# A two-layer transformer block with routed feed-forward on one core: routing steps moved, normalisation steps paired, a subtraction moved behind the statistics

## The chip, the cores and the metric

The kernel runs on one core of a Trainium2 chip. The metric is device microseconds of one execution; the kernel before takes 4644.64 us (median of three runs, 4642.4 to 4648.78). The core has five engines that each take their own instructions in order: TensorE (PE, with weight loads as PEld), VectorE (DVE), ScalarE (ACT), GpSimd (POOL) and SyncE (SP, which here only starts transfers). An engine that waits for something holds up everything written behind it for the same engine.

## The reference, cut to what matters

Two attention layers and two feed-forward layers alternate on x, 2048 tokens of 1024 numbers:

```python
x = x + A(layernorm(x));  x = x + B(layernorm(x))     # and the same two once more
# A: 32 heads of 32, full softmax attention over 2048 tokens, then @ wo
# B: r = x @ w_r; the 8 tokens with the largest r go through
#    y = (silu(x_sel @ w_gate) * (x_sel @ w_up)) @ w_down;  y *= sigmoid(r_sel)
#    result: x, with y added in the 8 rows
```

## The kernel before

Tokens lie in 16 tiles of 128 rows. `layer(n, ...)` is written once and run for n = 0 and n = 1. It has three stages: the projection to q, k and v (`steps`), the attention loop, and the output projection (`for t in range(NT)` at L1141), which also computes the layer norm that B needs and the router's score per token. Matrix products that need accuracy are made of three products of a high and a low part: ACT casts the high part, and DVE or POOL subtracts it from the whole to get the low one.

**The output projection.** For each tile t, PE makes 48 products (L1157) into a two-bank PSUM tile `pre`, of which there are two. DVE then adds the residual (L1168), scales the attention output of tile t+2 (`scale_o`, L1093), subtracts its low part (`split_o`, L1102, which waits for ACT's cast L1101), takes statistics (`ln_stats`, L141 to L146; the last two instructions, the reciprocal root `rs`, are POOL's), normalises (L1188) and makes the router's score (L1192). L1192 writes its unused product into `pre`, so the buffer comes free only when it is done. POOL makes the factors that are stored for later (L1182 to L1185) and adds x and its normalised value (L1193). At t = 0 DVE also makes the reciprocals of the second half of the softmax sums (L1002) in the memory that becomes `xn`.

**Routing of layer 0.** The feed-forward of layer 0 is spread over layer 1's projection. The 8 tokens are chosen in two stages, one over tiles 0 to 8 (`CT` = 9), one over the rest. Each is the generator `stage`, whose yields cut it in pieces; a piece is issued with `next`. The last piece computes positions `ab`, gathers 8 rows from DRAM with an indirect DMA on POOL's queue and scatters them to other rows of the same tensor, which moves the chosen rows to the end of their half. The first stage's pieces are issued inside the product loop of tiles 10, 11 and 12, the second stage's at steps k = 3 to 8 of layer 1's projection, one per step. At k = 9 the routed rows are normalised (L346) and transposed (L349) for the feed-forward. `permutation` (k = 13 and 17) multiplies three columns out to 8x8 tiles `vb` (L357), which PE transposes (L358).

**The hand-over.** Layer 1 is a generator too (`nxt`). While layer 0 finishes tiles 9 to 15, `next(nxt)` issues its first loads, the statistics and normalisation (`ln_stat`, `ln_norm`, L712) of its first four tiles, the split of its first weight block (`split_w`, cast L694, POOL's subtraction L697) and, after tile 15's products, the transposes of its first two tiles (`ln_tr`, L731, with the low parts on DVE, L739). Its loads of the tokens read the tensor that the scatter writes.

**Layer 1's projection.** Step k makes 24 products (L760), evacuated by ACT's cast (L774) and DVE's subtraction (L775) from three one-bank PSUM buffers `st`. Every second step splits the next weight block. In the first 24 steps, steps 8, 12, 16 and 20 also issue statistics and normalisation of a later tile. Every fourth step issues four pieces of the feed-forward (`tick`, L489 and L518) with the loads of its weights.

## Time and profile before

| | us |
|---|---|
| median of three runs | 4644.64 |
| profiled execution, time | 4644.15 |
| profiled execution, span from first to last instruction | 4642.1 |
| PE busy | 4520.6 (97%) |
| DVE, ACT, POOL busy | 3183.7, 2428.9, 3219.2 |
| mean granted TensorE clock | 0.988 |

An engine's timeline has one row for a run of like instructions: start, length, engine, line, operation, result and operands, and in brackets how long the engine had been idle before it and what ended that idle time. The chain that ended last says nothing here of the middle of the kernel, so the idle time of PE, which is busy 97% of the span, is the thing to read, stage by stage.

### The profile page before, as it was taken

How to read it: one execution, taken by the hardware profiler on the slowest of the kernel's cores; microseconds unless marked ns; L12 is line 12 of the kernel's file. 1: busy time of each engine (PE TensorE's matmuls, PEld its weight loads, DVE VectorE, ACT ScalarE, POOL GpSimd, SP SyncE). 2: the span in 40 equal slices, each digit the busy share in tenths (PEclk: the TensorE clock that was granted, in tenths of full speed). 3: DMA queues.
4: the chain of work that ended last, by engine and by line, in shares of the span. 5: the costliest groups of instructions: out<-in, count | busy, mean ns of one | idle time of the engine just before them, and what ended most of it. 6: DMA issues, size and time to landing. Idle time of an engine off the chain costs nothing. (4 is left out here: it accounts for less than half of the span.)

```text
span 4642.1 us, 73520 instructions
## 1 busy us (share of the span) xinstructions
PE 4520.6 (97%) x29224; PEld 2688.0 (58%) x29224; DVE 3183.7 (69%) x4945; ACT 2428.9 (52%) x2568; POOL 3219.2 (69%) x1247
## 2 busy tenths in 40 slices
PE   9999999999999999989899999999999999999896
PEld 7888755555555555448667786555555555554572
DVE  2211588888888888876422215888888888887763
ACT  3322267676767667750122222776676767677400
POOL 4444288988989898844433342988888899898441
PEclk9999999999999999999899999999999999999997
DMA  6757477776877777658489774777777768676597
GB/s 202 207 175 209 131 162 168 156 174 143 179 153 158 171 153 169 158 139 230 133 289 291 236 216 129 164 158 165 160 161 160 171 147 180 150 169 159 150 250 310
DMA packets 329301, 833.50 MB, mean 180 GB/s; under 512 B 44118, under 2 KB 159830, under 8 KB 279790
## 3 DMA queue, kind: packets, MB, share of 16 engines
q1 hardware_dynamic: 275214, 476.95, 35.0%
q0 software_dynamic: 45216, 325.57, 34.6%
q10 hardware_dynamic: 8528, 26.29, 2.2%
q8 instruction: 229, 3.75, 0.3%
q14 instruction: 114, 0.93, 0.1%
HBM read 384.24 MB, written 119.37 MB: 108 GB/s over the span
## 5 line engine op out<-in xcount | busy, mean ns | idle before, releaser
L639 DVE TENSOR_REDUCE nm<-st 128x1 f32<-128x512 f32 x3916 | 2433.7, 683 | 374.0 <-PE st L631 368.2
L1031 ACT ACTIVATE P<-pre 128x1024 f32<-128x1024 f32 x2048 | 1986.2, 1022 | 720.8 <-PE pre L646 522.2
L967 POOL TENSOR_TENSOR acc<-acc,P 128x2048 f32<-128x2048 f32 x434 | 2103.8, 4848 | 80.4 <-DMA P<-P 72.5
L646 PE MATMUL pre<-q,ks 64*128 64x512 f32 (+1 forms) x8192 | 1142.7, 396 | 4.3 <-ACT P L1031 4.3
L957 PE MATMUL pv<-P,v 128*32 128x512 f32 x8192 | 1091.9, 605 | 5.1 <-DMA v<-vd 5.1
L631 PEld LDWEIGHTS st<-ks,q 64*128 64x128 f32 x3916 | 546.5, 184 | 906.6 <-DVE nm L639 764.7
L631 PE MATMUL st<-ks,q 64*128 64x512 f32 x3916 | 980.6, 469 | 0.4
L646 PEld LDWEIGHTS pre<-q,ks 64*128 64x128 f32 (+1 forms) x8192 | 770.8, 186 | 190.7 <-ACT P L1031 57.4
L970 POOL DMA_DIRECT2D P<-P x310 | 296.4, 956 | 264.1 <-PE st L631 193.0
L775 DVE TENSOR_TENSOR lo<-st,hi 128x512 fp32r<-128x512 f32 x128 | 88.5, 691 | 568.4 <-ACT hi L774 562.7
L697 POOL TENSOR_TENSOR ohl<-wraw,ord 128x2048 fp32r<-128x2048 f32 x48 | 220.6, 4597 | 338.0 <-ACT ord L694 329.4
L697 POOL TENSOR_TENSOR wl<-wraw,wh 128x2048 fp32r<-128x2048 f32 (+1 forms) x49 | 221.1, 4512 | 303.8 <-ACT wh L694 285.0
L774 ACT CAST hi<-st 128x512 fp32r<-128x512 f32 x128 | 75.4, 589 | 564.1 <-PE st L760 564.1
L957 PEld LDWEIGHTS pv<-P,v 128*32 128x32 f32 x8192 | 161.8, 108 | 261.6 <-issue 253.3
L967 POOL TENSOR_TENSOR acc<-P 128x2048 f32<-128x2048 f32 x62 | 294.7, 4753 | 9.1 <-ACT P L1031 9.1
L1157 PE MATMUL pre<-woh,ohl 128*128 128x512 f32 x1024 | 245.3, 398 | 25.9 <-DVE pre L1192 14.4
L1157 PEld LDWEIGHTS pre<-woh,ohl 128*128 128x128 f32 x1024 | 195.9, 192 | 72.5 <-issue 17.2
L760 PE MATMUL st<-xh,wh 128*128 128x512 f32 x512 | 201.2, 393 | 0.0
L760 PE MATMUL st<-xh,wl 128*128 128x512 f32 x512 | 199.5, 390 | 0.0
L760 PE MATMUL st<-xl,wh 128*128 128x512 f32 x512 | 199.3, 389 | 0.0
L1101 ACT CAST ohl<-ord 128x1024 fp32r<-128x1024 f32 x32 | 33.6, 1051 | 309.6 <-DVE ord L1093 184.7
L760 PE MATMUL st<-woh,ord 128*128 128x512 f32 x512 | 166.8, 401 | 0.0
(344 smaller groups left out, 3866.7 us busy)
## 6 DMA issues: line engine op xcount, KB each, us to landing
P<-P POOLq DMA_DIRECT2D x310, 1024.0 KB, 8.8
wraw<-in_A_wqkv_dram SPq DMA_DIRECT2D x96, 1024.0 KB
q<-qh SPq DMA_DIRECT2D x256, 128.0 KB
ks<-kh SPq DMA_DIRECT2D x112, 256.0 KB
vd<-vn SPq DMA_DIRECT2D x32, 512.0 KB
qh<-hi SPq DMA_DIRECT2D x64, 256.0 KB
ql<-lo SPq DMA_DIRECT2D x64, 256.0 KB
kh<-hi SPq DMA_DIRECT2D x64, 256.0 KB
```

Source lines behind the costliest of these rows:

```text
L631: pe.matmul(ps[b], Q[u][rows, i, 0, qt * 128:(qt + 1) * 128], KS[(u // QC) % 2][rows, i, 0, j * 512:(j + 1) * 512], start=True, stop=True, ...
L639: dve.tensor_reduce(NM[u][:, j, 2 * i + b:2 * i + b + 1, qt], ps[b], axis=AX.X, op=OP.max, negate=True)
L646: pe.matmul(p[:, b * 512:(b + 1) * 512], KS[(u // QC) % 2][rows, i, slot, kt * 128:(kt + 1) * 128], Q[u][rows, i, slot, :], start=(slot == ...
L697: pool.tensor_tensor(wl[:, sl], raw[:, sl], wh[:, sl].bitcast(F32), op=OP.subtract)
L760: pe.matmul(p, *pair(a, l, r), start=(a == 0 and k == 0), stop=(a == KD - 1 and k == 2))
L774: act.copy(hi, p)
L775: dve.tensor_tensor(lo, p, hi.bitcast(F32), op=OP.subtract)
L957: pe.matmul(PV[u][32 * h:32 * h + 32, :], V[g][:, kt, 32 * h:32 * h + 32], P[s][:, h, :], start=(kt == 0), stop=(kt == NT - 1), tile_posit ...
L967: (dve if on_dve else pool).tensor_tensor(o, a, P[u * NT + k].rearrange("p h c -> p (h c)"), op=OP.add)
L970: pool.dma_start(P[u * NT + a], P[u * NT + b], accum_op=OP.add)
L1031: act.activation(P[s][:, 2 * i:2 * i + 2, :].rearrange("p h c -> p (h c)"), p, AF.Exp, scale=SCALE)
L1157: pe.matmul(p[:, bl], l[:, a, :], r[a][:, bl], start=(k == 0 and a == 0), stop=(k == 2 and a == KD - 1))
```

## The change

1. `stage` yields once more: the gather is issued in one piece, the scatter in the next. The first stage's pieces start one tile earlier (tile 9, last of the loop, then tiles 10, 11, and 12 at its third part's start), and the scatter is issued at tile 12 after the statistics. In the second stage the scatter comes at k = 9 and the routed rows at k = 10, so the feed-forward's pieces (`tick`, `refill`) come one step later too.
2. `permutation` makes `vb` on DVE.
3. `split_o` casts at once, and DVE's subtraction L1102 is issued after `ln_stats`, in both layers.
4. In the hand-over the statistics of layer 1's tiles 0 and 1 are issued together at tile 13, behind that tile's own statistics, their normalisations at its end; those of tiles 2 and 3 likewise at tile 14. Nothing is left of them at tile 15.
5. In layer 1 the low part of the first two weight blocks is subtracted in four instructions instead of one.
6. The small tiles `bst`, `mv` and `rs` are three deep instead of two, and an unused tile `pad` is shorter by 32 columns.

```diff
-        st = small.tile([128, 2, 6], F32, name="bst")
+        st = small.tile([128, 2, 6], F32, name="bst", bufs=3)      # mv and rs likewise
...
             self.gather(tg, abi[:, 0:1], dst)
-            self.scatter(abi[:, 1:2], tg, dst)
...
+            yield
+            self.scatter(abi[:, 1:2], tg, dst)
...
-                pool.tensor_scalar(vb, ones_c[:, 0:8], PERM[i]["v"][:, j:j + 1], None, op0=OP.mult)
+                dve.tensor_scalar(vb, ones_c[:, 0:8], PERM[i]["v"][:, j:j + 1], None, op0=OP.mult)
...
-                for i in range(parts):
-                    sl = slice(2048 // parts * i, 2048 // parts * (i + 1))
+                sls = [slice(2048 // parts * i, 2048 // parts * (i + 1)) for i in range(parts)]
+                for sl in [slice(0, 2048)] if n else []:
                     act.copy(wh[:, sl], raw[:, sl])
-                    if n:
-                        yield
+                    yield
+                for sl in sls:
+                    if not n:
+                        act.copy(wh[:, sl], raw[:, sl])
                     pool.tensor_tensor(wl[:, sl], raw[:, sl], wh[:, sl].bitcast(F32), op=OP.subtract)
...
                 ln_stat(0)
+                ln_stat(1)
+                yield
                 ln_norm(0)
-                yield
-                first_w = split_w()
+                ln_norm(1)
+                first_w = split_w(4)
                 next(first_w)
                 yield
-                ln_stat(1)
-                ln_norm(1)
-                yield
+                ln_stat(2)
+                ln_stat(3)
                 list(first_w)
                 load_w(blocks[2][1])
                 yield
-                ln_stat(2)
-                ln_stat(3)
                 ln_norm(2)
                 ln_norm(3)
...
-                    list(split_w())
+                    list(split_w(4 if n else 1))
...
-                    if k % 4 == 2 and k >= 10:
+                    if k % 4 == 3 and k >= 11:
                         for _ in range(4):
                             prev.tick()
-                    if k % 4 == 3:
+                    if k % 4 == 0:
                         prev.refill()
...
                 act.copy(oh, raw)
-                dve.tensor_tensor(ol, raw, oh.bitcast(F32), op=OP.subtract)
+                def low():
+                    dve.tensor_tensor(ol, raw, oh.bitcast(F32), op=OP.subtract)
+                return low
...
-                        if first_stage and t > CT and k == 2 and a in (0, 6):
+                        if first_stage and k == 2 and (t - CT, a) in ((0, 7), (1, 0), (1, 6), (2, 0), (2, 6), (3, 0)):
                             next(first_stage, None)
-                        if nxt and t >= NT - 3 and (k, a) == (2, 0):
-                            next(nxt)
...
-                if nxt and t in (NT - 4, NT - 1):
+                if nxt and t == NT - 1:
                     next(nxt)
...
-                if t + 2 < NT:
-                    split_o(t + 2)
+                low = split_o(t + 2) if t + 2 < NT else None
...
-                if nxt and t >= NT - 2:
+                if nxt and t == NT - 1:
                     next(nxt)
                 mv, rs = ln_stats(x2)
+                if low:
+                    low()
+                if first_stage and t == CT + 3:
+                    list(first_stage)
+                    next(nxt)
+                if nxt and NT - 3 <= t < NT - 1:
+                    next(nxt)
...
                 dve.scalar_tensor_tensor(waste, xn, 1.0, wrb, op0=OP.mult, op1=OP.mult, accum_out=rcols[:, t:t + 1])
+                if nxt and NT - 3 <= t < NT - 1:
+                    next(nxt)
...
-                if nxt and t in (CT, NT - 3):
+                if nxt and t == CT:
                     next(nxt)
```

More of the change, by code (lines that the diff above doesn't have):

```diff
@@ L98, in tile_kernel @@
     pool.memset(mone, -1.0)
-    cons.tile([128, 48], F32, name="pad")
+    cons.tile([128, 16], F32, name="pad")
     ones32 = cons.tile([128, 32], F32, name="ones32")
@@ L138, in ln_stats @@
     def ln_stats(xt):
-        st = small.tile([128, 2, 6], F32, name="bst")
+        st = small.tile([128, 2, 6], F32, name="bst", bufs=3)
         for i in range(2):
             dve.bn_stats(st[:, i, :], xt[:, i * 512:(i + 1) * 512])
-        mv = small.tile([128, 2], F32, name="mv")
+        mv = small.tile([128, 2], F32, name="mv", bufs=3)
         dve.bn_aggr(mv, st)
-        rs = small.tile([128, 1], F32, name="rs")
+        rs = small.tile([128, 1], F32, name="rs", bufs=3)
         pool.tensor_tensor(rs, mv[:, 1:2], eps_c, op=OP.add)
@@ L310, in stage @@
             dve.tensor_tensor(ab[:, 1:2], ab[:, 1:2], tcol, op=OP.add)
-            abi = perm["ab"] = cons.tile([8, 2], I32, name=f"ab{i}")
+            abi = cons.tile([8, 2], I32, name=f"ab{i}")
             dve.tensor_copy(abi, ab)
@@ L320, in stage @@
             else:
+                perm["ab"] = abi
                 dve.tensor_copy(v[:, 0:1], s)
+            yield
+            self.scatter(abi[:, 1:2], tg, dst)
         def absolute(self, out, pos2):
@@ L1126, in layer @@
                     store_sum(NU - 1, last_sum, rest[:, 512:1024])
-                    split_o(0)
+                    split_o(0)()
                 eng = pool if a in (4, 6) else dve
                 eng.tensor_tensor(wol[a], WOR[:, a, :], woh[a].bitcast(F32), op=OP.subtract)
-            split_o(1)
+            split_o(1)()
             second = XN[0:64, 0:512]
```

## The prediction

> **What bounds the kernel.** I read the page first, then who made PE wait in the two stretches around the output projections (2030 to 2560 us, 4260 to 4642 us), then the timelines of each engine there.

> ```profile
> span 4642.1 us, 73520 instructions
> PE 4520.6 (97%) x29224; PEld 2688.0 (58%) x29224; DVE 3183.7 (69%) x4945; ACT 2428.9 (52%) x2568; POOL 3219.2 (69%) x1247
> ...
> PE st L349 <- DVE fw L346: 11.1, 1, 11.1
> PE st L358 <- POOL vb L357: 9.9, 4, 4.6
> PE pre L1157 <- DVE pre L1192: 8.1, 3, 3.8
> PE st L731 <- DVE woh L739: 7.2, 1, 7.2
> PE st L235 <- DVE fy L232: 1.6, 1, 1.6
> PE pv L489 <- ACT fy L497: 1.2, 1, 1.2
> ...
> PE pre L1157 <- DVE pre L1192: 6.3, 4, 2.8
> ```

> PE idles only 121 us of 4642 (4642.1 - 4520.6). The first six waits (total, times, longest) lie in the first stretch, the last row in the second. The change touches nothing in the attention loop, so its gain must come out of about 45 us of waits, and of what follows a wait: a slower PE.

> ```profile
> 2047.58 3.92 PE L1157 MATMUL pre<-woh,ohl 128*128 128x512 f32 x16 [2.42 <-DVE ohl L1102]
> 2069.81 9.13 PE L1157 MATMUL pre<-woh,ohl 128*128 128x512 f32 x32 [3.81 <-DVE pre L1192]
> ...
> 2147.68 7.42 PE L1157 MATMUL pre<-woh,ohl 128*128 128x512 f32 x32
> ...
> 2158.56 7.42 PE L1157 MATMUL pre<-woh,ohl 128*128 128x512 f32 x32
> ...
> 2209.53 9.12 PE L1157 MATMUL pre<-woh,ohl 128*128 128x512 f32 x32 [2.56 <-DVE pre L1192]
> ...
> 2223.97 7.52 PE L1157 MATMUL pre<-woh,ohl 128*128 128x512 f32 x32 [1.70 <-DVE pre L1192]
> ...
> 2243.63 1.12 PE L731 MATMUL st<-ident,xt 128*128 128x128 f32 x4 [7.20 <-DVE woh L739]
> ```

> An undisturbed tile takes PE 10.88 us (2158.56 - 2147.68). The same 32 products take 7.42 us after no wait, 7.52 after 1.70 us, but 9.12 after 2.56 us: a wait of 2.56 us or more costs 1.7 us on top. After 2.42 us, 16 products took 3.92, little over half of 7.42. The price starts between 2.42 and 2.56 us, and I count half of it (0.85) for a wait that I forecast at about 2.5. [...]

> **DVE in one tile.**

> ```profile
> 2149.02 1.22 DVE L1093 TENSOR_TENSOR ord<-ord 128x1024 f32<-128x1024 f32 x1
> 2151.41 1.23 DVE L1102 TENSOR_TENSOR ohl<-ord,ohl 128x1024 fp32r<-128x1024 f32 x1 [1.17 <-ACT ohl L1101]
> 2152.55 1.28 DVE L141 BATCH_NORM_STATS2 bst<-x 128x6 f32<-128x512 f32 x2
> ...
> 2155.01 0.81 DVE L1188 TENSOR_SCALAR xn<-x,mv,rs 128x1024 f32<-128x1024 f32 x1 [0.93 <-POOL rs L146]
> 2155.86 1.23 DVE L1192 SCALAR_TENSOR_TENSOR pre<-xn,wrb 128x1024 f32<-128x1024 f32 x1
> ...
> 2158.76 1.23 DVE L1168 TENSOR_TENSOR x<-pre,x 128x1024 f32<-128x1024 f32 x1 [1.61 <-PE pre L1157]
> ```

> From one L1168 to the free buffer DVE needs about 9.3 us (L1168 and L1093 1.15 each from start to start, the wait, and 5.7 from 2151.41 to L1192's end), of which 1.17 is a wait for the cast and 0.93 one for POOL's root. Behind the statistics, the subtraction finds the cast done, and the root can run beside it: 7.2 to 8.1 us. I take 8, because POOL and DVE hold each other up (below). Against 10.88 us of PE this is hidden in ordinary tiles before and after: worth nothing in tiles 3 to 9. It counts only where DVE is late.

> **Tile 0's reciprocal.**

> ```profile
> 2059.86 3.34 DVE L1002 RECIPROCAL xn<-xn 64x512 f32<-64x512 f32 x1
> ...
> 2067.52 0.81 DVE L1188 TENSOR_SCALAR xn<-x,mv,rs 128x1024 f32<-128x1024 f32 x1 [2.95 <-DMA rd<-xn]
> ```

> L1188 overwrites the memory that L1002's result is being stored from, and waits 2.95 us for that store. With L1102 (1.15) and its wait (1.2) behind it, the reciprocal starts 2.35 us earlier, the store too, and PE's 3.81 us at tile 2 becomes about 1.5, short enough not to slow the clock: 2.35 + 1.65 = **4.0**. The second layer has the same wait, 2.8 us at most (the longest of its row); of it 1.3 to 2.4 goes, by whether the store or PE is last: **1.9**.

> **Tiles 10 to 15 of layer 0.**

> ```profile
> 2198.15 0.95 POOL L209 DMA_INDIRECT fw<-x,ab  x1 [1.48 <-DVE v L321]
> 2205.44 0.89 POOL L213 DMA_INDIRECT x<-fw,ab  x1 [6.34 <-DMA fw<-x,ab]
> ...
> 2207.24 0.81 DVE L1188 TENSOR_SCALAR xn<-x,mv,rs 128x1024 f32<-128x1024 f32 x1 [3.78 <-POOL rs L146]
> ...
> 2208.00 1.74 SPq L78 DMA_DIRECT2D xt<-x  x4
> ...
> 2211.37 1.29 DVE L141 BATCH_NORM_STATS2 bst<-xt 128x6 f32<-128x512 f32 x2 [1.99 <-DMA xt<-x]
> ...
> 2226.90 4.60 POOL L697 TENSOR_TENSOR ohl<-wraw,ord 128x2048 fp32r<-128x2048 f32 x1
> ...
> 2226.97 5.08 DVE L712 TENSOR_SCALAR xt<-xt,mv,rs 128x1024 f32<-128x1024 f32 x1 [1.76 <-POOL rs L146]
> ...
> 2242.16 0.81 DVE L712 TENSOR_SCALAR xt<-xt,mv,rs 128x1024 f32<-128x1024 f32 x1 [0.44 <-POOL rs L146]
> ```

> At tile 10, PE waits 1.6 us for a piece that was issued only 12 products earlier; spread by one tile, the piece finds its inputs made, unless a small DVE operation is held by POOL: **1.0** (0 to 1.6).

> At tile 12, POOL stands 6.34 us in front of the scatter, and tile 12's root is queued behind it. So L1188 is 3.78 us late, and PE waits 2.56 us at tile 14. Now the root comes first, and only POOL's store factors and L1193 wait. The wait and its slow clock go: 2.56 + 1.7 = **4.3**.

> At tile 13, DVE took layer 1's first statistics and normalisation ahead of L1168, with 1.99 us waiting for the load, and PE waits 1.70 us at tile 15. Now two statistics stand between tile 13's statistics and its L1188, so the buffer comes free about 8 + 3 = 11 us after the products end, against 10.88. L1193, delayed behind the scatter, may add 0.5. **1.1** of 1.7 goes. The statistics need the loads in time. Set the end of tile 12's products to 0: the gather's issue starts at about 0, the scatter 7.3 us later (2205.44 - 2198.15), the loads another 2.56 (2208.00 - 2205.44), the first tile lands 3.4 later (2211.37 - 2208.00): 13.3. DVE comes to it at about 10.9 + 5 = 15.9: a margin of 2.6 us.

> At tile 15, PE makes 12 of 16 transposes and waits 7.20 us for the low part (L739), because DVE first does statistics and normalisation of tiles 2 and 3, up to 2242.16 + 0.8, behind a tile 14 that was itself late (5.08 us for an L712 of 0.81 that lay beside POOL's 4.60 us L697). DVE holds still until POOL's instruction ends. In four pieces of 1.15 us, I take it that POOL and DVE take turns: tile 14's L1192 and the two L712 each wait for one piece, 3.5 us together, hardly less than one wait of 4.3. What gains is the order. Counted from the end of tile 13's products: L1168 of tile 14 at 12, four statistics halves each for three tiles to 17.7, then L1188, L1192 and two L712 with three pieces between them to 25. Tile 15's products end at 21.8, the 12 transposes at 23.3, the low part is there at 25.7: PE waits 2.4, or 3.0 with the 0.6 of tile 13. 4.2 to 4.8 goes, and half a slow clock: **5.3**. Without any turn-taking the wait would be gone, with a slow clock of 1.7 (8.9); if POOL goes first throughout, 2 less. [...]

> **Steps 8 to 10 of layer 1.**

> ```profile
> 2299.93 0.59 ACT L774 CAST hi<-st 128x512 fp32r<-128x512 f32 x1 [2.88 <-PE st L760]
> ...
> 2303.28 4.50 POOL L697 TENSOR_TENSOR ohl<-wraw,ord 128x2048 fp32r<-128x2048 f32 x1
> ...
> 2308.60 0.81 DVE L712 TENSOR_SCALAR xt<-xt,mv,rs 128x1024 f32<-128x1024 f32 x1 [11.65 <-POOL rs L146]
> 2309.33 0.68 DVE L775 TENSOR_TENSOR lo<-st,hi 128x512 fp32r<-128x512 f32 x1
> ...
> 2310.18 0.80 DVE L346 TENSOR_SCALAR fw<-bg,mg 8x1024 f32<-8x1024 f32 x1
> ```

> L346 stands behind step 8's L712, which waits 11.65 us for a root behind POOL's weight subtraction, which stands behind the scatter. With the scatter one step later, the subtraction starts at once, the L712 ends within step 9, and at step 10 PE waits only for the chain that always follows a step's end: cast 0.59, L775 0.68, two tiny operations 0.25, L346 0.80, with gaps 2.45. 11.14 - 2.45 = 8.7, and half a slow clock: **9.5** (8.7 to 10.4).

> **Moves on DVE.**

> ```profile
> 2344.60 1.30 POOL L357 TENSOR_SCALAR vb<-ones,v 8x8 f32<-8x8 f32 x3
> ...
> 2344.65 0.82 DVE L712 TENSOR_SCALAR xt<-xt,mv,rs 128x1024 f32<-128x1024 f32 x1 [6.68 <-POOL rs L146]
> ```

> The 9.9 us look like POOL's, but at 2344.60 DVE had itself been idle for 6.68 us for the same root. On DVE, `vb` is queued behind that L712 and that L775, 1.45 us after the root instead of at once. Three tiny operations, I estimate, take DVE about 0.4 us less than POOL's 1.30 takes with its hand-offs to PE. The later tick takes three loads of 1 MB out of the way of the weight block of steps 12 and 16, which should start the cast up to 1.5 us earlier. Net **1.6** for both places (-2 to 3).

> **Second layer's tiles.**

> ```profile
> 4486.30 1.22 DVE L1102 TENSOR_TENSOR ohl<-ord,ohl 128x1024 fp32r<-128x1024 f32 x1 [3.71 <-ACT ohl L1101]
> ```

> DVE's waits for the cast are longer there, up to this one, and the shorter chain behind a late cast (no statistics, no root) frees the buffer 2.4 us earlier. Of the remaining 3.5 us (6.3 - 2.8) I count **3.0** (2 to 3.5); the transfers are no shorter.

> **The sum.** 4.0 + 1.9 + 1.0 + 4.3 + 1.1 + 5.3 + 9.5 + 1.6 + 3.0 = 31.7. The profiled execution took 4644.15 us, 2.05 more than its span, and lies 0.5 under the median of the runs; 4644.64 - 31.7 = **4613**.

> **Rivals.** *The moves cost nothing at all.* If `vb` finds DVE free, both waits (9.9) and two slow clocks (3.4) go instead of 1.6: 4613 - 11.7 = 4601. Against it stands the 6.68 us row. Chance 0.12.

> *The loads come late at tile 13.* If gather, scatter and load take over 2.6 us longer than in the rows, DVE stands still with tile 13's buffer in hand, PE loses what it gained at tiles 15 and after (1.1 + 5.3) and gets a new slow clock (1.7): 4621, and up to 4628 where the delay is 10 us. For it: SP issues the loads ahead of that tile's stores, and POOL's queue is in order. Chance 0.15.

> *Slower: the later ticks stall PE.* In two thirds of the projection the 13 ticks now fall on the steps that transpose a tile. If there each waited 2.6 us for a buffer and paid 1.7 of slow clock, 13 x 4.3 = 56 us would be lost: 4669. It decides from 31.7 / 13 = 2.4 us a tick. Against it: before, one wait of 1.2 us (L489) is the only one of its kind, and the steps that ticks leave carry the weight casts. Chance 0.04.

> *It does not do what it says.* The moves on DVE and the four pieces may relieve nothing; that is counted above.

> **How the numbers follow.** The forecast's cluster, 25 to 40 us gained, has 0.66; the rivals 0.12, 0.15 and 0.04; 0.03 is left for a change that does nothing. The range takes in the first two rivals and the bounds of the terms: 4598 to 4630. A measurement of this kernel tells 0.2%, 9 us, from no change: faster 0.92, same 0.03, slower 0.05.

> **What would show it.** Right: L349 waits about 2.5 us on L346; L731 2 to 3 on L739; L358's wait is as long as before but names DVE, with L712 and L775 in front of it; no wait on L1192 at tile 14; the second layer's row falls from 6.3 to under 2. Wrong: L358 without a wait, L141 waiting for `xt` at tile 13, or new PE waits between 2350 and 2650 us.

## The result, and the profile after

The changed kernel takes 4604.83 us (median of four runs, 4602.4 to 4608.43) beside 4645.48 us for the kernel before (four runs, 4642.4 to 4648.78): a ratio of 0.9913, 95% interval 0.9896 to 0.993. The forecast was 4613 us, range 4598 to 4630. The gain is 41 us (32 to 48 by the interval) where 31.7 were summed. The profiled execution took 4602.4 us, span 4600.4; by spans the gain is 41.7 us, and every place below is read from that pair.

The page of the changed kernel, and then its waits on PE between 2025 and 2530 us and, for the last row, from 4220 us on (who waited, for whom; us in total, times, longest). Lines have shifted: L1192 of before is L1202, L731 and L739 are L735 and L743, L349 and L346 are L351 and L348, L358 and L357 are L360 and L359, L712 is L716, L697 is L701, L1188 is L1198, L1102 is L1107.

```profile
span 4600.4 us, 73517 instructions
PE 4509.8 (98%) x29224; PEld 2687.3 (58%) x29224; DVE 3174.4 (69%) x4951; ACT 2429.3 (53%) x2568; POOL 3239.3 (70%) x1247
...
PE st L360 <- DVE vb L359: 8.5, 4, 4.1
PE st L351 <- DVE fw L348: 2.4, 1, 2.4
PE st L735 <- DVE woh L743: 0.5, 1, 0.5
PE pre L1161 <- DVE pre L1202: 0.3, 1, 0.3
...
PE pre L1161 <- DVE pre L1202: 0.3, 1, 0.3
```

Beside the rows of before: L358's 9.9 us has become L360's 8.5 and names DVE; L349's 11.1 has become 2.4; L731's 7.2 has become 0.5; the router's row has gone from 8.1 to 0.3 in the first stretch and from 6.3 to 0.3 in the second.

PE's timeline in the changed kernel: tile 2, tiles 14 and 15, the hand-over's transposes, the routed rows' transposes, and the moves with the two products behind them.

```profile
2064.87 7.54 PE L1161 MATMUL pre<-woh,ohl 128*128 128x512 f32 x32 [0.25 <-DVE pre L1202]
...
2199.22 7.42 PE L1161 MATMUL pre<-woh,ohl 128*128 128x512 f32 x32
2210.10 7.42 PE L1161 MATMUL pre<-woh,ohl 128*128 128x512 f32 x32
2220.99 1.47 PE L735 MATMUL st<-ident,xt 128*128 128x128 f32 x12
2222.99 0.66 PE L735 MATMUL st<-ident,xt 128*128 128x128 f32 x4 [0.53 <-DVE woh L743]
...
2285.19 0.66 PE L351 MATMUL st<-ident,fw 8*128 8x8 f32 x8 [2.37 <-DVE fw L348]
...
2311.15 0.33 PE L360 MATMUL st<-ident,vb 8*8 8x8 f32 x4 [4.06 <-DVE vb L359]
...
2312.78 1.05 PE L764 MATMUL st<-woh,ord 128*128 128x512 f32 x2
```

Tiles 14 and 15 wait for nothing and follow each other in 10.88 us (2210.10 - 2199.22), as an undisturbed tile does. The eight transposes behind the 2.37 us wait take 0.66 us, where before, behind 11.14 us, they took 1.02, and the granted clock stays at 1.00 behind them: no slow clock is left there. Behind 4.06 us there is one: two products take 1.05 us instead of 0.62.

Where the 41.7 us of span came from, by the starts of the same PE rows in both traces, beside the terms of the prediction:

| place | forecast | gained |
|---|---|---|
| start of layer 0's output projection | 0 | 1.4 |
| its first product to tile 3 (the reciprocal) | 4.0 | 5.1 |
| tiles 3 to 8 | 0 | 0.0 |
| tiles 9 to 12 | 1.0 | 1.0 |
| tiles 13 to 15 | 5.4 | 6.4 |
| end of tile 15 to tile 2's transposes | 5.3 | 8.6 |
| from there to step 12 of layer 1's projection | 9.5 | 11.0 |
| from there to step 20 (the two permutations) | 1.6 | 1.8 |
| second layer's tiles | 4.9 | 6.9 |
| the rest | 0 | -0.5 |

### The profile page after: what moved, and what is told of

It is laid out like the page before. It is cut to its first block, busy times and chain, and to the rows that moved or that the text cites. A ratio compares the mean times of both kernels' runs of the same rounds, so it can differ in the third digit from the quotient of the medians.

```text
span 4600.4 us, 73517 instructions
## 1 busy us (share of the span) xinstructions
PE 4509.8 (98%) x29224; PEld 2687.3 (58%) x29224; DVE 3174.4 (69%) x4951; ACT 2429.3 (53%) x2568; POOL 3239.3 (70%) x1247
## 5 line engine op out<-in xcount | busy, mean ns | idle before, releaser
L779 DVE TENSOR_TENSOR lo<-st,hi 128x512 fp32r<-128x512 f32 x128 | 88.5, 691 | 561.0 <-ACT hi L778 551.5
L701 POOL TENSOR_TENSOR ohl<-wraw,ord 128x2048 fp32r<-128x2048 f32 (+1 forms) x54 | 222.2, 4120 | 336.5 <-ACT ord L696 318.3
L701 POOL TENSOR_TENSOR wl<-wraw,wh 128x2048 fp32r<-128x2048 f32 (+1 forms) x49 | 221.2, 4514 | 304.2 <-ACT wh L700 275.0
L1161 PE MATMUL pre<-woh,ohl 128*128 128x512 f32 x1024 | 241.7, 393 | 11.0 <-ACT ohl L1104 5.8
L1161 PEld LDWEIGHTS pre<-woh,ohl 128*128 128x128 f32 x1024 | 194.1, 190 | 55.0 <-ACT ohl L1104 7.7
```

The costliest lines, as they stand in the source:

```text
L701: pool.tensor_tensor(wl[:, sl], raw[:, sl], wh[:, sl].bitcast(F32), op=OP.subtract)
L779: dve.tensor_tensor(lo, p, hi.bitcast(F32), op=OP.subtract)
L1161: pe.matmul(p[:, bl], l[:, a, :], r[a][:, bl], start=(k == 0 and a == 0), stop=(k == 2 and a == KD - 1))
```

## The experiments

All ratios are to the kernel before, measured on the same chip, where it took 4650 to 4653 us. The changed kernel itself was not timed there: below, a ratio is set against its 0.9913 and against the 0.9907 of the run with the moves on POOL; 0.001 is 4.7 us. An interval reaches 0.0012 to 0.0017 to either side, 6 to 8 us: smaller differences rest on the traces. On the chip of the last four runs (e9 to e12) no kernel was timed that could stand in for the changed one.

To read the traces against each other, this table cuts each profiled execution at four starts on PE: the output projection of layer 0, the transposes behind tile 15, the output projection of layer 1, and the first product behind it (L441). Its last column is the time from there to the end.

| kernel | to projection 0 | projection 0 | to projection 1 | projection 1 | end |
|---|---|---|---|---|---|
| before | 2039.7 | 195.2 | 2115.0 | 194.3 | 97.9 |
| changed | 2038.4 | 182.6 | 2094.5 | 187.4 | 97.5 |
| e1 moves on POOL | 2038.4 | 184.1 | 2097.7 | 195.0 | 94.6 |
| e2 one piece | 2039.4 | 184.0 | 2098.9 | 193.5 | 99.5 |
| e3 scatter with gather | 2042.2 | 184.0 | 2103.4 | 189.9 | 96.3 |
| e4 subtract first | 2040.7 | 193.9 | 2097.4 | 200.5 | 99.1 |
| e5 moves early | 2052.2 | 183.5 | 2083.2 | 187.4 | 94.7 |
| e6 routed rows early | 2052.8 | 184.2 | 2077.0 | 189.4 | 95.7 |
| e7 old hand-over | 2039.5 | 190.9 | 2097.3 | 191.3 | 97.6 |
| e8 subtract last, alone | 2039.9 | 186.9 | 2113.4 | 189.8 | 97.3 |
| e9 moves early, same places | 2039.2 | 183.9 | 2084.3 | 193.5 | 97.2 |
| e10 routed rows early, same places | 2038.6 | 185.0 | 2077.4 | 193.7 | 96.6 |
| e11 pad of before | 2051.0 | 182.7 | 2095.9 | 189.6 | 99.0 |
| e12 pad 8 columns longer | 2054.1 | 184.3 | 2092.7 | 189.9 | 96.5 |

The column of projection 1 is noisy: eleven kernels that have the changed kernel's code there lie between 187.4 and 195.0. PE's waits on the router's row differ with it: 0.3 us in the changed kernel, 0.2 to 4.9 in the ten others (3.8 in e2 and e10, 4.9 in e1). The changed kernel's trace is one of the two shortest.

**The moves back on POOL.**

```diff
-                dve.tensor_scalar(vb, ones_c[:, 0:8], PERM[i]["v"][:, j:j + 1], None, op0=OP.mult)
+                pool.tensor_scalar(vb, ones_c[:, 0:8], PERM[i]["v"][:, j:j + 1], None, op0=OP.mult)
```

> The changed kernel with the 8x8 tiles vb made on POOL again, all else kept. Theory A (the moves gain nothing by being on DVE: DVE's normalisation and the subtraction of the step stand in front of them, and POOL is free as soon as the root is made): PE waits at L360 7 to 9 us in all as now (8.5), the time within 2 us of the changed kernel (4604.8), rather 1 to 2 us faster, because vb no longer stands behind 1.45 us of DVE work. Theory B (the move to DVE is what shortened the stall): 2 us slower or more, up to 10.

4606.97 us, 0.9907 (0.9894 to 0.992), the changed kernel's own ratio. The wait of L360 names POOL again. First the row of this run, then the rows of the changed kernel on DVE:

```profile
PE st L360 <- POOL vb L359: 7.0, 4, 3.4
```

```profile
2309.55 0.81 DVE L716 TENSOR_SCALAR xt<-xt,mv,rs 128x1024 f32<-128x1024 f32 x1 [5.12 <-POOL rs L146]
2310.28 0.68 DVE L779 TENSOR_TENSOR lo<-st,hi 128x512 fp32r<-128x512 f32 x1
2310.88 0.34 DVE L359 TENSOR_SCALAR vb<-ones,v 8x8 f32<-8x8 f32 x2
```

On DVE the broadcast stands behind L716 and L779, as forecast, and both engines stand behind the same root: DVE had been idle for 5.12 us when it came. The wait is 1.5 us longer on DVE than on POOL. Moving the moves gains nothing. Steps 12 to 20 of layer 1's projection take 66.6 us in the changed kernel and 66.5 here in spite of the shorter waits: the clock behind the two places runs at half for 10.2 us in the changed kernel and for 13.7 here.

**The first split in one piece.**

```diff
-                first_w = split_w(4)
+                first_w = split_w()
...
-                    list(split_w(4 if n else 1))
+                    list(split_w())
```

> The changed kernel with the low part of the first two weight blocks of layer 1 in one instruction each again. Theory A (in the trace of the changed kernel POOL started its pieces only after tile 14's L1202, and only the last normalisation met them; with one piece of 4.6 us that one waits for all of it): the second L716 of tile 15's preparation lasts 4 to 5 us, PE waits 2.5 to 3.5 us at L735 instead of 0.5, time 2 to 4.5 us more. Theory B (the pieces relieve nothing, as the prediction counted): within 1 us of 4604.8.

4616.01 us, 0.9924 (0.9911 to 0.9937): 5 to 8 us over the changed kernel, with intervals that overlap, where 2 to 4.5 were expected. In the trace of this run, POOL's piece, DVE's normalisation and the hand-over's transposes:

```profile
2221.30 5.76 DVE L716 TENSOR_SCALAR xt<-xt,mv,rs 128x1024 f32<-128x1024 f32 x2
2221.76 4.76 POOL L701 TENSOR_TENSOR ohl<-wraw,ord 128x2048 fp32r<-128x2048 f32 x1
...
2227.72 1.11 PE L735 MATMUL st<-ident,xt 128*128 128x128 f32 x4 [2.80 <-DVE woh L743]
```

The same rows of the changed kernel, with the root behind which POOL was held:

```profile
2217.03 1.24 DVE L1202 SCALAR_TENSOR_TENSOR pre<-xn,wrb 128x1024 f32<-128x1024 f32 x1
2217.12 1.91 POOL L146 TENSOR_TENSOR rs<-rs,mhalf 128x1 f32<-128x1 f32 x1
2218.18 2.51 DVE L716 TENSOR_SCALAR xt<-xt,mv,rs 128x1024 f32<-128x1024 f32 x2
2218.64 5.67 POOL L701 TENSOR_TENSOR ohl<-wraw,ord 128x512 fp32r<-128x512 f32 x4
```

Whole, the subtraction holds the second of DVE's two L716 until its own end (the pair takes 5.76), PE waits 2.80 us, and the clock turns slow (four transposes 1.11 instead of 0.66). In pieces the pair takes 2.51, beside one piece. From tile 15 to tile 2's transposes this run takes 3.9 us more than the changed kernel (20.07 against 16.17, from 2212.48 to 2232.55 and from 2210.10 to 2226.27), and 1.1 more in a wait of tile 15. So the pieces are worth about 5 us in their place.

**The scatter in the gather's piece.**

```diff
             self.gather(tg, abi[:, 0:1], dst)
+            self.scatter(abi[:, 1:2], tg, dst)
...
             yield
-            self.scatter(abi[:, 1:2], tg, dst)
```

> The changed kernel with the scatter issued in the same piece as its gather again, in both stages; everything else, the later ticks too, stays. Theory A (POOL standing in front of the scatter held the weight subtraction and the roots queued behind it): L348 waits 9 to 11 us instead of 2.4, the clock slows behind it, and tile 14 of layer 0 waits 1 to 2 us again: 10 to 13 us more. Theory B (the later step of the feed-forward alone hides the chain): within 2 us of 4604.8.

4618.89 us, 0.9935 (0.9923 to 0.9948): 10 to 13 us over the changed kernel. In this run's trace the scatter, the subtraction and the normalisation stand in a row in front of the routed rows:

```profile
2285.13 0.88 POOL L213 DMA_INDIRECT x<-fw,ab  x1 [6.08 <-DMA fw<-x,ab]
2286.04 4.54 POOL L701 TENSOR_TENSOR ohl<-wraw,ord 128x2048 fp32r<-128x2048 f32 x1
...
2291.41 4.99 DVE L716 TENSOR_SCALAR xt<-xt,mv,rs 128x1024 f32<-128x1024 f32 x1 [11.77 <-POOL rs L146]
...
2298.62 1.02 PE L351 MATMUL st<-ident,fw 8*128 8x8 f32 x8 [10.60 <-DVE fw L348]
```

This is the picture of before again: 10.60 us of wait and a slow clock in place of 2.37 and none. The stretch to projection 1 is 8.9 us longer than the changed kernel's, as the step of the prediction has it (9.5). In layer 0 the earlier scatter costs only a wait of 1.1 us, at tile 14 (projection 0 is 1.4 longer).

**The subtraction ahead of the statistics.**

```diff
-                low = split_o(t + 2) if t + 2 < NT else None
+                if t + 2 < NT:
+                    split_o(t + 2)()
...
-                if low:
-                    low()
```

> The changed kernel with DVE's subtraction L1107 ahead of the statistics again, right behind the scaling (and the reciprocal of tile 0 behind it). Theory A (three places gain from the order: tile 2 in both layers, by the reciprocal's store, and the second layer's tiles with late casts): PE's waits on the score at L1161 come back, 3.8 and 2.8 us at tile 2 and 3 to 4 in the second layer's later tiles, 5.1 + 2.5 + 4.3 = 12 us more, 10 to 14. Theory B (only the late casts matter): 4 to 5 us more.

4632.41 us, 0.996 (0.9948 to 0.9972): 22 to 25 us over the changed kernel, more than any other part and about twice the 10 to 14 of its expectation. Projection 0 is 11.3 us longer than the changed kernel's and projection 1 13.1 (5.5 more than the longest of the eleven). In this run's trace, tile 5 of layer 1 shows what the forecast had only as a remainder (ACTq is the time ACT spends on issuing loads):

```profile
4378.68 12.22 ACTq L1085 DMA_DIRECT2D ord<-rd  x4
4391.00 1.05 ACT L1104 CAST ohl<-ord 128x1024 fp32r<-128x1024 f32 x1 [13.99 <-DMA ord<-rd]
4392.08 1.22 DVE L1107 TENSOR_TENSOR ohl<-ord,ohl 128x1024 fp32r<-128x1024 f32 x1 [5.38 <-ACT ohl L1104]
...
4397.96 0.76 PE L1161 MATMUL pre<-woh,ohl 128*128 128x512 f32 x1 [2.78 <-DVE pre L1201]
```

ACT is busy for 12.22 us with issuing four loads, so its cast starts late, DVE waits 5.38 us for it with this tile's statistics still to come, and PE waits 2.78 us for the buffer. With the subtraction behind the statistics, the statistics and the root are made while the cast is late.

**The moves a step early, and the routed rows too.** The broadcasts get a step of their own one step ahead of the transposes, in three buffers; the second kernel also normalises the routed rows a step ahead.

```diff
+        def moves(self, i):
...
-                vb = small.tile([8, 8], F32, name="vb")
+                vb = small.tile([8, 8], F32, name="vb", bufs=3)
...
-                    if k in (13, 17):
-                        prev.permutation(k // 17)
+                    if k in (14, 18):
+                        prev.moves(k // 18)
+                    if k in (15, 19):
+                        prev.permutation(k // 19)
...
-            yield      # second kernel only: ahead of the routed rows' normalisation
...
+            yield      # behind it, ahead of the transposes
```

> The changed kernel, but the three broadcasts of the moves (L359) are made in a step of their own, one step ahead of the small transposes that use them (steps 14 and 18, transposes at 15 and 19), in three buffers. Theory A: TensorE's waits on L360 (8.5 us in four) and the slow clock behind the two long ones (about 1.7 each) vanish, and nothing later takes their place: 10 to 12 us under the changed kernel. Rival B: the broadcasts were only the last of a chain that is late anyway, and the stall goes to the next reader of the small transposes: within 3 us of the changed kernel.

> As the run before, and the routed rows' normalisation is issued one step ahead of the transposes that read it (with the scatter, at step 9; transposes at step 10). Theory A: the 2.4 us wait of L351 on L348 vanishes too: 2 to 3 us under the run before. Rival B: the wait is for the gathered rows to land, so it stays at 2.4 or moves to VectorE, and the time is that of the run before within 1.5 us.

4607.21 us, 0.991 (0.9894 to 0.9925), and 4602.26 us, 0.9898 (0.9883 to 0.9913). By its time the first, expected 10 to 12 us under the changed kernel, would be the rival's; the second is 5 us under the first, where 2 to 3 were expected. By its trace the first is not the rival's: PE has no wait of the moves' transposes at all, and the stretch to projection 1 is 11.3 us shorter than the changed kernel's; with the routed rows early 17.5 us, and the wait of L351 is gone too. Steps 12 to 20, where the moves stand, take 53.3 us in both, 13.3 less than in the changed kernel. But both kernels reach projection 0 some 14 us later (2052.2 and 2052.8 against 2038.4), in a stretch of which nothing was edited. Groups of PE rows by shape, up to 560 us, first of the changed kernel, then of the first of the two (count, busy us, mean ns of one):

```profile
L764 PE MATMUL st<-xh,wl 128*128 128x512 f32 x512 | 199.5, 390 | 0.4 <-POOL wl L701 0.4
L764 PE MATMUL st<-xl,wh 128*128 128x512 f32 x512 | 199.3, 389 | 0.0
```

```profile
L770 PE MATMUL st<-xl,wh 128*128 128x512 f32 x512 | 202.3, 395 | 0.0
L770 PE MATMUL st<-xh,wl 128*128 128x512 f32 x512 | 202.2, 395 | 0.0
```

The same products take 395 ns instead of 389, at a granted clock of 1.00 from 200 to 400 us in both. Over some 2,200 of them that is 13 us. The third buffer had moved every tile allocated behind it by 32 bytes.

**The old hand-over.**

```diff
                 ln_stat(0)
-                ln_stat(1)
-                yield
                 ln_norm(0)
-                ln_norm(1)
+                yield
                 first_w = split_w(4)
...
+                        if nxt and t >= NT - 3 and (k, a) == (2, 0):
+                            next(nxt)
...
-                if nxt and NT - 3 <= t < NT - 1:
-                    next(nxt)
```

> The changed kernel, but with the hand-over's steps in the order and at the places of the kernel before (statistics and normalisation of the next layer's first tiles in pairs, the first split between them, advanced at the same tiles and products as before). The split stays in four pieces. Theory A: the order is what freed tiles 13 to 15: waits of TensorE on the router's line at tile 14 and on L743 come back, 6 to 12 us over the changed kernel. Rival B: the pieces alone do it: within 3 us of the changed kernel.

4615.81 us, 0.9926 (0.9912 to 0.9939), 6 to 9 us over the changed kernel; projection 0 is 8.3 us longer. The waits on PE of this run, and the row of DVE behind the first of them:

```profile
PE pre L1164 <- DVE pre L1203: 5.9, 2, 5.7
PE st L735 <- DVE woh L743: 2.4, 1, 2.4
```

```profile
2206.10 1.29 DVE L141 BATCH_NORM_STATS2 bst<-xt 128x6 f32<-128x512 f32 x2 [6.46 <-DMA xt<-x]
```

DVE takes layer 1's first statistics ahead of tile 13's residual, as before, and waits 6.46 us for the load, where before it waited 1.99; the 5.7 us wait of PE is that of tile 15. So the order matters beside the pieces, and the new place of the scatter needs the new place of the statistics: the loads follow the scatter. The paired work out of tile 15 shows in L735's 2.4 against 0.5.

**The subtraction behind the statistics, alone,** in the kernel before.

```diff
                 act.copy(oh, raw)
-                dve.tensor_tensor(ol, raw, oh.bitcast(F32), op=OP.subtract)
+
+                def low():
+                    dve.tensor_tensor(ol, raw, oh.bitcast(F32), op=OP.subtract)
+                return low
...
                 mv, rs = ln_stats(x2)
+                if low:
+                    low()
```

> The kernel before with one part of the change: the subtraction L1102 issued after the tile's statistics. Theory A: this is the part that takes ScalarE's casts, late behind the issuing of loads, off the chain from a tile's product to its store; it gives 10 to 25 us against the kernel before, as much as undoing it in the changed kernel cost. Rival B: the part gives the forecast's share only, 7 to 9 us (tile 2 of both layers and tile 10), and the rest of what undoing it cost belongs to its meeting with the other parts.

4632.23 us, 0.9963 (0.9949 to 0.9976): 11 to 24 us of gain from this part alone, by the table 8.3 in projection 0 and 4.5 in projection 1 against the profiled kernel before. It leaves all the other stalls as they were; the waits on PE of this run:

```profile
PE st L349 <- DVE fw L346: 11.3, 1, 11.3
PE st L731 <- DVE woh L739: 7.2, 1, 7.2
PE pre L1160 <- DVE pre L1196: 4.5, 2, 2.5
```

**The places of the tiles.** An unused tile `pad` lies among the constants. The change made it 32 columns (128 bytes) shorter. In the first pair of runs it is made 8 columns shorter still, which takes up the third broadcast buffer; in the second pair the kernel is the changed one but for the length of `pad`.

```diff
-    cons.tile([128, 16], F32, name="pad")
+    cons.tile([128, 8], F32, name="pad")      # early moves, early routed rows
...
+    cons.tile([128, 48], F32, name="pad")     # pad of before
...
+    cons.tile([128, 24], F32, name="pad")     # 8 columns longer
```

> The run with the moves' broadcasts a step early again, with the unused tile pad shorter by 8 columns, the 32 bytes of the third broadcast buffer, so that every tile allocated behind lies where it lies in the changed kernel. In the run without that, the stall of L360 was gone and the stretch from L351 to the second layer's output projection 11.2 us shorter, but the first layer's projection products took 395 ns each instead of 389, 14 us in all. Theory A: the products are slower because their tiles lie 32 bytes further on; back in their old places they take 389, and the whole kernel is 10 to 12 us under the changed kernel. Rival B: the products are slower for another reason (the instruction stream): within 3 us of the run without the shorter pad.

> The run with the routed rows' normalisation a step early too, with the same shorter pad. Theory A: first layer's products at 389 ns, no wait of L351, no wait of the moves: 12 to 15 us under the changed kernel, the fastest of all. Rival B: products stay at 395, the time is that of the run without the shorter pad within 3 us.

> The changed kernel with pad at its old 48 columns, so that the deeper small tiles push everything behind them 128 bytes further on. Theory A: the shorter pad is a working part of the change: without it the first layer's projection products take more than 389 ns, 5 to 20 us over the changed kernel. Rival B: only 32-byte steps that are no multiple of 64 or 128 matter: within 3 us of the changed kernel.

> The changed kernel with pad 8 columns longer, so that everything behind it lies 32 bytes further on, and no other difference. Theory A: the places alone make the first layer's projection products 395 ns: 12 to 16 us over the changed kernel. Rival B: within 3 us of it, and the slower products belong to the edited code.

4599.23 us, 0.9884 (0.9868 to 0.9899); 4593.93 us, 0.9875 (0.9859 to 0.989); 4618.61 us, 0.9927 (0.9913 to 0.994); 4619.38 us, 0.9927 (0.9913 to 0.994). The first two reach projection 0 at 2039.2 and 2038.6 again, the last two at 2051.0 and 2054.1, with not one instruction changed. The groups up to 560 us, of the early moves in their old places, then of `pad` of before and of `pad` 8 columns longer:

```profile
L770 PE MATMUL st<-xl,wh 128*128 128x512 f32 x512 | 199.2, 389 | 0.0
```

```profile
L764 PE MATMUL st<-xl,wh 128*128 128x512 f32 x512 | 202.2, 395 | 0.0
L764 PE MATMUL st<-xl,wh 128*128 128x512 f32 x512 | 202.3, 395 | 0.0
```

So where the tiles lie sets what these products take, and the shorter `pad` is a working part of the change: without it the changed kernel reaches projection 0 12.6 us later. By the ratios the last two lose 7 to 9 us, with intervals that overlap the changed kernel's; this is less than their stretch shows and than their expectation had (12 to 16 for the last); where the difference comes back is not settled, and the noise of the last columns is of that size. The shorter `pad` takes 12 us off the early moves (0.991 to 0.9884), and 11 off the early routed rows. The fastest kernel of all is the changed one with moves and routed rows a step early and `pad` at 8 columns, 4593.93 us.

## Why the prediction was right, point by point

The total came out within the range, and the waits that were to go went, with their causes as forecast at tile 2, at tiles 13 to 15, at steps 8 to 10 and in the second layer. Three things did not hold: how POOL and DVE share the hand-over, what DVE saves at the moves, and the price of a wait in slow clock. The sizes were low nearly throughout, 31.7 against 41.7, one term was missing, and part of the 41.7 is luck of this trace, as said below.

**Tile 2** (4.0, measured 5.1). In DVE's timeline of the changed kernel:

```profile
2056.05 3.34 DVE L1005 RECIPROCAL xn<-xn 64x512 f32<-64x512 f32 x1
...
2062.58 0.81 DVE L1198 TENSOR_SCALAR xn<-x,mv,rs 128x1024 f32<-128x1024 f32 x1 [0.72 <-POOL rs L146]
```

The reciprocal starts 2.4 us earlier against the first product (2056.05 - 2038.35 = 17.7, before 2059.86 - 2039.74 = 20.1), 2.35 forecast. But L1198 no longer waits for the store: it starts at most 3.2 us behind the reciprocal's end, before 4.3. So PE's wait fell to 0.25 us. The step mis-sized is "becomes about 1.5", for want of a shorter store. The second layer shows the same wait of 0.25, with 2.5 us gained, 1.9 forecast.

**Tiles 9 to 12** (1.0, measured 1.0): the wait of 1.6 us on L232 is gone, and a new one of 0.6 us, L250 on L246, took part of the gain, the small DVE operation that the term allowed for. **Tiles 13 to 15** (5.4, measured 6.4): no wait at tile 14 or 15, as the prediction's signs said. The rival of loads that come late at tile 13 did not come; e7 shows its stall where the order is the old one.

**The hand-over** (5.3, measured 8.6) is the term furthest off. The step that failed is "I take it that POOL and DVE take turns", with three waits of a piece each. In the rows of the changed kernel POOL's pieces begin at 2218.64, after tile 14's L1202, because POOL itself had been held in its root (L146, 1.91 us, where two others of this tile took 0.55) beside that L1202. Only L716 met a piece, 2.51 us for the two. So the low part was there 0.5 us after PE asked for it, where the signs had 2 to 3, and the slow clock went whole. The prediction's own alternative, no turn-taking (8.9), came closer than its term. The sentence that the pieces gain "hardly" against the order fell too: e2 puts them at about 5 us in their place, and e7 the order at 6 to 9 us. The 8 us for DVE's tile rest on no row of before that has the root beside the subtraction; in the changed kernel's tile at 2141 us the root was held there (1.06 us instead of 0.19, the last section), and DVE took 7.7 us from the start of L1172 to the end of L1202 (2149.02 - 2141.35).

**Steps 8 to 10** (9.5, measured 11.0). The wait came to 2.37 us, 2.45 forecast. The term was low because half a slow clock was counted for it, and none came. That none came is luck: the same wait of 2.37 us stands in eight other runs, and behind it the clock slowed in six of them (e1, e2, e4, e5, e9, e11). From the start of step 8 to that of step 12 the projection takes 29.9 us in the changed kernel, e7 and e12, 31.4 to 31.5 in e1, e2, e9 and e11, and 33.0 in e4 and e5. With 40.9 before, the gain there is 11.0, 9.4 or 7.9 us; half a slow clock was a fair count.

**The moves** (1.6, measured 1.8) are right in sum and wrong in a part. The stall stayed and named DVE, with L716 and L779 in front, as said. But of the two parts, the tiny operations, said to save 0.4 on DVE, cost 1.5 (7.0 on POOL, 8.5 on DVE); what the pair gained came from elsewhere, and e1's time is no worse. A shorter slow clock is part of it: 10.2 us behind the two places, 13.7 before. Whether the later tick had a share was only argued. The rival "the moves cost nothing at all" (4601) described what e5 and e9 then did by another edit: with the broadcasts a step early the two stalls and their slow clocks, 13.3 us of steps 12 to 20, are gone. The whole stretch is 10 to 11 us shorter, in part because the clock slowed behind L351's wait in both runs and not in the changed kernel.

**Second layer's tiles** (3.0, measured 4.4 behind tile 3). The reason, a shorter chain behind late casts, held: e4, without it, waits 8.5 us on the router's row there. But the size is the upper end: the row fell from 6.3 to 0.3 in this trace, and lies above the sign's 2 in six of the ten others with the same code. And the reason was costed only here and at tile 2: e4 and e8 put the whole part, over both layers, at 17 to 25 us. Of tiles 9 to 15 of layer 0 it has a share that the forecast gave to the other parts.

**The slow clock.** The step "The price starts between 2.42 and 2.56 us" failed as a rule for a single wait: in e4 the clock was slow behind a wait of 1.82 us and one of 0.58 right after it, and in e8 one of 2.47 us left it alone (the last section shows, for the 2.37 us of L351, where the wait fell in two runs). In the changed kernel neither of the two waits forecast at about 2.5 us was followed by a slow clock, for different reasons: at the hand-over the wait was 0.5 us, and at step 10 it fell luckily.

**The missing term.** The prediction did not mention `pad`. It was taken for bookkeeping of memory; e11 puts at 7 us (by time, with intervals that overlap) to 13 us (in the stretch to projection 0) what it kept from being lost. The forecast came out right because it silently assumed what `pad` was there to bring about.

## What to carry to other kernels

When a tile is made deeper, look at what moves behind it: compare the mean time of products in a part of the kernel that the edit does not touch, before blaming the edit. An operation that waits for a slow neighbour belongs behind those that do not need it, on the engine whose queue holds the buffer; here that one line was worth more than any move of work between engines. And a wait that names an engine is no reason to move the work to another one, when both stand behind the same third thing: move it in time instead. Last, a forecast that prices a slow clock behind a wait of 2 to 2.5 us should carry it as a chance.

## What the runs showed of the hardware

**Places of tiles.** 128x512 products of layer 0's projection took 389 ns or 395 ns by where their tiles lay, 32 or 128 bytes apart. Products of layer 1's projection did not show it (`pre<-ord,woh` 390 ns in the changed kernel and in e5). Whether it is the stationary tile, the moving one or both was not tried. Whether these products wait for an engine or a transfer, or are slower by themselves, no run here shows.

```profile
2281.11:2284.52 3.41, 1.71 (x8) 1.09 (x6) 1.37 (x5) 1.66 (x3) 0.56 (x1) 1.00 0.40 111
2284.53:2287.94 3.41, 2.75 (x17) 2.37 (x18) 0.83 (x2) 0.80 (x1) 2.52 (x1) 1.00 0.98 221
2287.94:2291.35 3.41, 3.41 (x16) 2.77 (x15) 0.00 (x0) 0.00 (x0) 2.07 (x1) 1.00 0.72 216
```

```profile
2284.66:2288.08 3.42, 1.05 (x11) 0.75 (x10) 1.70 (x5) 2.47 (x3) 0.54 (x1) 1.00 0.76 224
2288.08:2291.49 3.41, 3.41 (x9) 2.64 (x10) 0.15 (x1) 0.00 (x0) 3.41 (x1) 0.50 0.97 205
```

In the changed kernel such a point cuts the wait into 1.70 and 0.66 us; in e9 the whole of it lies in one stretch, and the next 3.41 us run at half clock. In e7 the slowing began behind the first rows after a wait: four transposes behind 2.44 us took their 0.66 us, and 1.5 us after their start, at 2235.85, one product took 0.63 us instead of 0.39.

**DVE and POOL.** The first half of a root (L145, 128 numbers) on POOL took 1.06 us beside DVE's subtraction and 0.19 us without it. The row of the changed kernel with the subtraction it lay beside, and one without:

```profile
2145.06 1.17 DVE L1107 TENSOR_TENSOR ohl<-ord,ohl 128x1024 fp32r<-128x1024 f32 x1
2145.22 1.06 POOL L145 TENSOR_TENSOR rs<-mv,eps_c 128x1 f32<-128x1 f32 x1 [4.68 <-DVE mv L143]
...
2205.82 0.19 POOL L145 TENSOR_TENSOR rs<-mv,eps_c 128x1 f32<-128x1 f32 x1 [0.84 <-DVE mv L143]
```

So the postponed subtraction does lengthen the root: this row is 0.87 us longer, and it ends 0.05 us behind the DVE instruction (2146.28 and 2146.23). DVE then waits 0.71 us for the root, in a tile where PE waits for nothing.
